# One MLP kernel, its first microseconds: x in two loads on two queues, w1's first half behind them, products by tiles

## The chip, the cores and the metric

The kernel runs on one core of a Trainium2 chip. The metric is the device time of one execution, in microseconds (us). Times are given as the median of several runs; the profile is of one further execution. Engines are named as in the profile: PE is TensorE's matmul and PEld its weight load, DVE is VectorE, ACT is ScalarE, POOL is GpSimd and SP is SyncE. A name with a q behind it (SPq, ACTq) is the engine's instruction stream, as it issues DMAs.

## The reference

```python
B, S, D, F = 1, 2048, 512, 1792        # bf16 inputs x, w1, b1, w2

def reference(x, w1, b1, w2):
    h = jnp.einsum("bsd,df->bsf", x, w1) + b1
    sp = jnp.log1p(jnp.exp(-jnp.abs(h))) + jnp.where(h > 0, h, jnp.zeros_like(h))
    act = h * jnp.tanh(sp)
    return jnp.einsum("bsf,fd->bsd", act, w2)
```

Two matrix products with a Mish activation between them: 2048 rows, 512 columns in, 1792 in the middle, 512 out.

## The kernel before

It is written by hand, engine by engine: each engine executes its instructions in the order in which the code issues them, and `Stream.wait` puts a semaphore wait ahead of an engine's next instruction. `load` issues one DMA with a semaphore of its own and returns the token to wait for; `load_w1` and `load_part` load columns of w1 for some of its four 128-row slices, k 0 to 3.

The 2048 rows are cut into four blocks of 512 (`BLOCKS`), a block into four tiles of 128 rows. The first product needs x with its columns on the partitions (`xT`). Its 512 columns are the four slices k, its 1792 outputs are fourteen slices f of 128. For block s and slice f, four matmuls (k 0 to 3) of 512 columns add up in one PSUM bank, ScalarE applies Mish with the bias and writes `a_sb` (`mish`, L160), and when a block's fourteen slices are done, `mm2` (L199) multiplies each of its four row tiles by w2 in fourteen matmuls; VectorE copies the result out of PSUM (L205) and SP stores it. The first products are those of L177.

Block 0 is started differently, and the change lies there. Of its four tiles, 2 and 3 come already transposed by a DMA (`t_x23`). Tiles 0 and 1 come as they are into `x_nat`, in one load of 256 KB from SP (`t_xn`), in which partition p holds rows 2p and 2p+1, so tile 0 holds the even rows and tile 1 the odd ones; the stores of these two tiles put them back (`rows`). TensorE transposes them in eight 128 x 128 pieces, tile by slice (`transpose_x`, L147), in four groups, each into a PSUM bank, and VectorE and ScalarE take turns to copy the groups into `xT` (L151).

Until x has landed, TensorE runs nine fillers (`WARM`, `dummy`, L130): matmuls of constants into a bank that nobody reads, five of 512 columns, three of 256 and one of 128. Behind the transposes come the products of slices f 0 to 3 (`F0` = 4) in banks 4 to 7, by `first(js, ks)` with row tiles js and slices ks:

```python
first((0,), (0,))
first((1,), (0,))
first((0, 1), range(1, KT))
first((2, 3), range(KT))
```

Each line runs over its ks, and within one k over the four slices f. Then follow slices 4 to 7 in two halves of k, each matmul 512 wide (`half`), and the rest.

The queues at the start: ScalarE issues w1's k 0-1 and k 2-3 for f 0 to 3 (256 KB each) ahead of its activation table; SP issues x, the DMA transpose of tiles 2 and 3, w1's columns for f 4 to 7 in two halves, b1, w1's columns for f 8 to 13, w2, and the DMA transposes of the other three blocks. A product waits for the load of its slice of w1 (`t_w1`) and for the copies or the DMA that made its part of `xT` (`t_cp`).

Of the kernel before, what the change touches and what calls it, by code (L numbers as in the profile page):

```python
# [4 lines left out]

P = 128
SQ = 32
WARM = (512,) * 5 + (256,) * 3 + (128,)
BLOCKS = (512, 512, 512, 512)


# [21 lines left out]
def bass_standalone__dense_activation_mish__prompt_kernel(  # L33
# [10 lines left out]
    BF, F32 = dt.bfloat16, dt.float32  # L44
# [3 lines left out]
    KT, FT = D // P, F // P  # L48
    assert (S, D, F) == (2048, 512, 1792) and sum(BLOCKS) == S
    x2, out2 = x[0], out[0]  # L50
# [3 lines left out]
    F0 = 4  # L54
    N0 = BLOCKS[0] // P

    with ExitStack() as es:
        def sb(name, shape, t):
            return es.enter_context(nc.sbuf_tensor(name, shape, t))

        x_nat = sb("x_nat", [P, 2, D], BF)
        xT = sb("xT", [P, KT, S], BF)
# [6 lines left out]
        ident = sb("ident", [P, P], BF)  # L69
        a_sb = sb("a_sb", [P, FT, S], BF)  # L70
        o_sb = sb("o_sb", [P, S // P, D], BF)
        ps = es.enter_context(nc.psum_tensor("ps", [P, 8, 512], F32))

        def sem(name):
            return es.enter_context(nc.semaphore(name))

        sp = Stream(nc.sync, None)
        pe = Stream(nc.tensor, sem("c_pe"))
        dve = Stream(nc.vector, sem("c_dve"))
        act = Stream(nc.scalar, sem("c_act"))  # L80
        pool = Stream(nc.gpsimd, sem("c_pool"))

        def load(q, dst, src, name, transpose=False):
            s = sem(name)
            (q.eng.dma_start_transpose if transpose else q.eng.dma_start)(dst, src).then_inc(s, 16)
            return (s, 16)

        def load_w1(q, ks, a, b):
            return load(q, w1_sb[:, ks, a * P:b * P], w1v[:, ks, a * P:b * P], "s_w1_%d_%d" % (ks.start, a))
# [5 lines left out]
        def load_part(q, k0, k1, a, b):  # L95
            t = load_w1(q, slice(k0, k1), a, b)
            for f in range(a, b):
                for k in range(k0, k1):
                    t_w1[k, f] = t

        t_bz = dve.mark(nc.vector.memset(b1_nat[:, :], 0.0))  # L101
        for k0, k1 in ((0, 2), (2, 4)):
            load_part(act, k0, k1, 0, F0)
        t_xn = load(sp, x_nat[:, :, :], x2[0:2 * P, :].rearrange("(p j) d -> p j d", p=P), "s_xn")
        t_x23 = load(sp, xT[:, :, 2 * P:4 * P], x2[2 * P:4 * P, :], "s_x23", True)
        for k0, k1 in ((0, 2), (2, 4)):
            load_part(sp, k0, k1, F0, 8)
# [3 lines left out]
        t = load(sp, w2_sb[:, :, :], w2v, "s_w2")  # L111
# [3 lines left out]
        for s in range(1, len(BLOCKS)):  # L115
            lo, hi = starts[s], starts[s + 1]
# [5 lines left out]
        t_id = pool.mark(pool.eng.affine_select(ident[:, :], ones[:, :], pattern=[[1, P]], compare_op=ALU.is_equal,  # L122
                                                fill=0.0, base=0, channel_multiplier=-1))
        act.eng.preload_act_table(ACT.Mish)  # L124

        c_w = nc.const_aps.tensor(1.0, [P, P], BF)
        c_m = nc.const_aps.tensor(1.0, [P, 512], BF)

        def dummy(n):
            nc.tensor.matmul(ps[:, 7, 0:n], c_w, c_m[:, 0:n], start=True, stop=True)  # L130


        free = [[] for _ in range(8)]
        t_cp = {(j, k): t_x23 for j in (2, 3) for k in range(KT)}
        t_mish, t_acc = {}, {}

        def transpose_x():

            pe.wait(t_xn, t_id)
            for bank, (eng, js, ks) in enumerate(((dve, (0,), (0,)), (act, (1,), (0,)), (dve, (0, 1), (1,)),  # L140
                                                  (act, (0, 1), (2, 3)))):
                n, m = len(ks), len(js)
                psb = ps[:, bank, 0:n * m * P // 2].bitcast(BF)
                for i, k in enumerate(ks):
                    for h, j in enumerate(js):
                        lo = (i * m + h) * P
                        mm = nc.tensor.transpose(psb[:, lo:lo + P], x_nat[:, j, k * P:(k + 1) * P], ident[:, :])  # L147
                eng.wait(pe.mark(mm))
                dst = xT[:, ks[0]:ks[0] + n, js[0] * P:(js[-1] + 1) * P]
                src = psb.rearrange("p (k t) -> p k t", k=n)  # L150
                t = eng.mark(nc.vector.tensor_copy(dst, src) if eng is dve else act.eng.activation(dst, src, ACT.Copy))  # L151
                for k in ks:
                    for j in js:
                        t_cp[j, k] = t
                free[bank] = [t]

        def mish(s, f, bank, t_mm):
# [7 lines left out]
        def mm1_step(s, f, k, bank, js=None):  # L165

            n = BLOCKS[s]
            lo, hi = (0, n) if js is None else (js[0] * P, (js[-1] + 1) * P)
            first = k == 0 and lo == 0
            if first:  # L170
                pe.wait(*free[bank])
            pe.wait(t_w1[k, f])
            if s:
                pe.wait(t_xT[s])
            else:
                pe.wait(*[t_cp[j, k] for j in (js or range(N0))])
            return nc.tensor.matmul(ps[:, bank, lo:hi], w1_sb[:, k, f * P:(f + 1) * P],  # L177
                                    xT[:, k, starts[s] + lo:starts[s] + hi], start=first, stop=(k == KT - 1 and hi == n))
# [6 lines left out]
        s_out = sem("s_out")  # L185
        n_out = 0

        def rows(i):

            if i < 2:  # L190
                return out2[0:2 * P, :].rearrange("(p j) d -> p j d", p=P)[:, i, :]
            return out2[i * P:(i + 1) * P, :]

        def mm2_step(i, f, lo, hi, bank):
            s = max(b for b in range(len(BLOCKS)) if starts[b] <= i * P)
            if f == 0:
                pe.wait(*free[bank])
            pe.wait(t_w2[f], t_mish[s, f])
            return nc.tensor.matmul(ps[:, bank, 0:hi - lo], a_sb[:, f, i * P:(i + 1) * P], w2_sb[:, f, lo:hi],  # L199
                                    start=(f == 0), stop=(f == FT - 1))  # L200

        def put(i, lo, hi, bank, t_mm):
            nonlocal n_out
            dve.wait(t_mm)
            t = dve.mark(nc.vector.tensor_copy(o_sb[:, i, lo:hi], ps[:, bank, 0:hi - lo]))  # L205
            free[bank] = [t]
            sp.wait(t)
            sp.eng.dma_start(rows(i)[:, lo:hi], o_sb[:, i, lo:hi]).then_inc(s_out, 16)
            n_out += 1

        def mm2(i, lo, hi, bank):
            for f in range(FT):
                mm = mm2_step(i, f, lo, hi, bank)
            put(i, lo, hi, bank, pe.mark(mm))


        def first(js, ks):
            for k in ks:
                for f in range(F0):
                    mm = mm1_step(0, f, k, 4 + f, js)  # L220
                    if k == KT - 1 and js[-1] == N0 - 1:
                        t_acc[f] = pe.mark(mm)
# [5 lines left out]
                if ks[-1] == KT - 1:  # L228
                    t_acc[f] = pe.mark(mm)

        for n in WARM:
            dummy(n)
        transpose_x()
        first((0,), (0,))
        first((1,), (0,))
        first((0, 1), range(1, KT))
        first((2, 3), range(KT))

        dve.wait(t_b1)
        for j in range(P // SQ):  # L240
            t = dve.mark(nc.vector.transpose(b1_T[j * SQ:(j + 1) * SQ, :], b1_nat[:, j * SQ:(j + 1) * SQ]))  # L241
# [52 lines left out]
```

## Time and profile before

| | |
|---|---|
| Runs (three) | 104.72 us median, 104.55 to 105.31 |
| Profiled execution | 105.42 us; span in the profile 104.1 us |
| PE | 101.5 us busy, 499 matmuls |
| ACT | 39.7 us busy; 48.0 us idle ahead of Mish, waiting for products |
| DVE | 12.8 us busy |
| DMA | 7.94 MB, 76 GB/s mean over the span |

A row of the timeline gives the start in us, the length in us, engine, line, operation, what is written and what is read, and how many instructions are merged (x8); in brackets the idle time ahead of them and what ended it. A row of the windows gives a stretch, its length, then the busy time and count of instructions of engines, the granted clock, the DMA engines' share and their GB/s. An answer on a tile has the line of each DMA that writes it, with its issue time in ns, its first and last issue in us, and the time from issue to landing.

### The profile page before, as it was taken

Reading aid. Unit: us, or ns where it says so; the run is one execution under the profiler, and the core shown is the slowest. Engines: PE = TensorE matmul, PEld = TensorE weight load, DVE = VectorE, ACT = ScalarE, POOL = GpSimd, SP = SyncE. Lnnn points to the kernel's source line nnn. Section 1 sums busy time; section 2 is a strip of 40 time slices with the busy share of each in tenths; the row PEclk is TensorE's granted clock in tenths of the full one; section 3 lists DMA queues with packets and bytes.
Section 4 is the critical chain, followed back from the end, with each engine's and each line's share of the span. In section 5 each row is a group of like instructions: output and inputs, shape, how many; then the busy total and the mean of one; then the engine's idle time right before and its main releaser. Section 6 shows DMA issues by size and latency. Waiting matters only on the chain.

```text
span 104.1 us, 1139 instructions
## 1 busy us (share of the span) xinstructions
PE 101.5 (97%) x499; PEld 48.8 (47%) x499; DVE 12.8 (12%) x25; ACT 39.7 (38%) x59; POOL 0.7 (1%) x6
## 2 busy tenths in 40 slices
PE   6999999999999999999999999999999999999992
PEld 2786444444444444444444444444444444444462
DVE  0103000022220000022220000022112000011223
ACT  3405997000027777200007777500005777700000
POOL 2000000000000000000000000000000000000000
PEclk9999999999999999999999999999999999999999
DMA  2999999681101000010111000001111000001111
GB/s 46 334 339 363 348 317 178 145 203 50 44 7 50 0 0 6 0 50 0 50 50 50 0 0 3 0 6 50 50 50 50 0 0 0 0 0 57 50 50 50
DMA packets 13345, 7.94 MB, mean 76 GB/s; under 512 B 7836, under 2 KB 13212, under 8 KB 13340
## 3 DMA queue, kind: packets, MB, share of 16 engines
q1 hardware_dynamic: 12796, 7.35, 27.1%
q10 hardware_dynamic: 544, 0.52, 1.4%
q8 instruction: 4, 0.07, 0.3%
q14 instruction: 1, 0.01, 0.0%
HBM read 3.94 MB, written 2.10 MB: 58 GB/s over the span
## 4 chain that ended last, share of the span: by engine, by line
PE 97%; DVE 0%; issue 0%
PE ps L177 47%; PE ps L199 46%; PE ps L130 3%; PE ps L147 1%; DVE o_sb L205 0%
## 5 line engine op out<-in xcount | busy, mean ns | idle before, releaser
L160 ACT ACTIVATE a_sb<-ps,b_sb 128x512 bf16<-128x512 f32 x56 | 37.5, 691 | 48.0 <-PE ps L177 48.0
L177 PE MATMUL ps<-xT,w_sb 128*128 128x512 bf16 (+2 forms) x244 | 49.8, 367 | 0.0
L199 PE MATMUL ps<-w_sb,a_sb 128*128 128x512 bf16 (+2 forms) x238 | 49.0, 366 | 0.0
L177 PEld LDWEIGHTS ps<-xT,w_sb 128*128 128x128 bf16 x244 | 24.2, 101 | 24.8
L199 PEld LDWEIGHTS ps<-w_sb,a_sb 128*128 128x128 bf16 x238 | 22.8, 98 | 25.9
L205 DVE CAST o_sb<-ps 128x512 bf16<-128x512 f32 (+2 forms) x17 | 11.2, 660 | 82.4 <-PE ps L199 82.4
L130 PE MATMUL ps<-const-bfloat16-1.0 128*128 128x512 bf16 (+2 forms) x9 | 3.0, 519 | 0.8 <-PEq L279 0.8
L130 PEld LDWEIGHTS ps<-const-bfloat16-1.0 128*128 128x128 bf16 x9 | 1.2, 138 | 2.3 <-issue 2.2
L124 ACT ACT_TABLE_LOAD x1 | 1.3, 1283 | 1.8 <-issue 1.8
L151 ACT ACTIVATE xT<-ps 128x128 bf16<-128x128 bf16 (+1 forms) x2 | 0.9, 437 | 1.4 <-PE ps L147 1.4
L241 DVE STREAM_TRANSPOSE b_T<-b_nat 32x32 bf16<-32x32 bf16 x4 | 0.8, 202 | 3.3 <-DMA b_nat<-in_b_dram 3.2
L147 PE MATMUL ps<-ident,x_nat 128*128 128x128 bf16 x8 | 1.0, 311 | 0.0
L151 DVE COPY xT<-ps 128x128 bf16<-128x128 bf16 (+1 forms) x2 | 0.5, 258 | 3.2 <-PE ps L147 3.1
L147 PEld LDWEIGHTS ps<-ident,x_nat 128*128 128x128 bf16 x8 | 0.8, 142 | 0.2 <-DMA x_nat<-in_x_dram 0.2
L122 POOL TENSOR_SCALAR_AFFINE_SELECT ident<-ones 128x128 bf16<-128x128 bf16 x1 | 0.3, 292 | 0.1
L101 DVE MEMSET b_nat<- 32x64 uint32 x1 | 0.1, 112 | 0.9 <-PEq L279 0.9
L120 POOL MEMSET ones<- 128x128 bf16 x1 | 0.2, 204 | 0.3 <-POOLq L279 0.3
L243 DVE CAST b_sb<-b_T 128x14 f32<-128x14 bf16 x1 | 0.2, 176 | 0.0
L279 POOL MEMSET const-bfloat16-1.0<- 128x1 bf16 x1 | 0.1, 101 | 0.0
L279 POOL MEMSET const-uint8-127<- 128x1 uint8 x1 | 0.1, 101 | 0.0
L279 POOL MEMSET const-float32-0.0<- 128x1 f32 x1 | 0.1, 98 | 0.3 <-issue 0.3
L279 POOL MEMSET const-float32-1.0<- 128x1 f32 x1 | 0.1, 99 | 0.0
## 6 DMA issues: line engine op xcount, KB each, us to landing
out_dram<-o_sb SPq DMA_DIRECT2D x15, 128.0 KB, 1.7
w_sb<-in_w_dram SPq DMA_DIRECT2D x1, 1792.0 KB, 10.3
w_sb<-in_w_dram SPq DMA_DIRECT2D x1, 768.0 KB, 5.5
w_sb<-in_w_dram ACTq DMA_DIRECT2D x2, 256.0 KB, 3.8
w_sb<-in_w_dram SPq DMA_DIRECT2D x2, 256.0 KB, 4.4
x_nat<-in_x_dram SPq DMA_DIRECT2D x1, 256.0 KB, 2.9
out_dram<-o_sb SPq DMA_DIRECT2D x1, 96.0 KB, 1.6
xT<-in_x_dram SPq DMA_TRANSPOSE x4, 5.9
```

Of the source, the lines that this page charges most:

```text
L120: t_ones = pool.mark(pool.eng.memset(ones[:, :], 1.0))
L122: t_id = pool.mark(pool.eng.affine_select(ident[:, :], ones[:, :], pattern=[[1, P]], compare_op=ALU.is_equal, fill=0.0, base=0, channel_mu ...
L124: act.eng.preload_act_table(ACT.Mish)
L130: nc.tensor.matmul(ps[:, 7, 0:n], c_w, c_m[:, 0:n], start=True, stop=True)
L147: mm = nc.tensor.transpose(psb[:, lo:lo + P], x_nat[:, j, k * P:(k + 1) * P], ident[:, :])
L151: t = eng.mark(nc.vector.tensor_copy(dst, src) if eng is dve else act.eng.activation(dst, src, ACT.Copy))
L160: t = act.mark(act.eng.activation(a_sb[:, f, starts[s]:starts[s + 1]], ps[:, bank, 0:n], ACT.Mish, bias=b1_sb[:, f:f + 1]))
L177: return nc.tensor.matmul(ps[:, bank, lo:hi], w1_sb[:, k, f * P:(f + 1) * P], xT[:, k, starts[s] + lo:starts[s] + hi], start=first, stop=( ...
L199: return nc.tensor.matmul(ps[:, bank, 0:hi - lo], a_sb[:, f, i * P:(i + 1) * P], w2_sb[:, f, lo:hi], start=(f == 0), stop=(f == FT - 1))
L205: t = dve.mark(nc.vector.tensor_copy(o_sb[:, i, lo:hi], ps[:, bank, 0:hi - lo]))
L241: t = dve.mark(nc.vector.transpose(b1_T[j * SQ:(j + 1) * SQ, :], b1_nat[:, j * SQ:(j + 1) * SQ]))
L279: nc = _bacc.Bacc("TRN2", target_bir_lowering=False, num_devices=1)
```

## The change

x's tiles 0 and 1 become two loads of 128 KB, rows 0 to 127 from SP and rows 128 to 255 from ScalarE. SP then issues w1's k 0-1 for f 0 to 3, and the DMA transpose third. ScalarE issues k 2-3 later, when the fourth filler (`HOLD` = 3, counted from 0) has finished. The fillers become five of 512 columns, one of 256 and two of 128. Each tile is transposed by itself when it is there, its slices 0 and 1 copied by VectorE, 2 and 3 by ScalarE. The products run over slices 0 and 1 of tile 0, then of tile 1, then over slices 2 and 3 of both. The rows of a tile are consecutive now, and `rows` goes.

```diff
-WARM = (512,) * 5 + (256,) * 3 + (128,)
+WARM = (512,) * 5 + (256,) + (128,) * 2
+HOLD = 3
...
-        for k0, k1 in ((0, 2), (2, 4)):
-            load_part(act, k0, k1, 0, F0)
-        t_xn = load(sp, x_nat[:, :, :], x2[0:2 * P, :].rearrange("(p j) d -> p j d", p=P), "s_xn")
+        t_xn = [load(q, x_nat[:, j, :], x2[j * P:(j + 1) * P, :], "s_xn%d" % j) for j, q in enumerate((sp, act))]
+        load_part(sp, 0, 2, 0, F0)
         t_x23 = load(sp, xT[:, :, 2 * P:4 * P], x2[2 * P:4 * P, :], "s_x23", True)
...
-        def transpose_x():
-
-            pe.wait(t_xn, t_id)
-            for bank, (eng, js, ks) in enumerate(((dve, (0,), (0,)), (act, (1,), (0,)), (dve, (0, 1), (1,)),
-                                                  (act, (0, 1), (2, 3)))):
...
+        def transpose_x(j):
+
+            pe.wait(t_xn[j], t_id)
+            for h, eng in enumerate((dve, act)):
+                bank = 2 * j + h
+                psb = ps[:, bank, 0:P].bitcast(BF)
+                for i in range(2):
+                    k = 2 * h + i
+                    mm = nc.tensor.transpose(psb[:, i * P:(i + 1) * P], x_nat[:, j, k * P:(k + 1) * P], ident[:, :])
                 eng.wait(pe.mark(mm))
-                dst = xT[:, ks[0]:ks[0] + n, js[0] * P:(js[-1] + 1) * P]
-                src = psb.rearrange("p (k t) -> p k t", k=n)
+                dst = xT[:, 2 * h:2 * h + 2, j * P:(j + 1) * P]
+                src = psb.rearrange("p (k t) -> p k t", k=2)
...
-            sp.eng.dma_start(rows(i)[:, lo:hi], o_sb[:, i, lo:hi]).then_inc(s_out, 16)
+            sp.eng.dma_start(out2[i * P:(i + 1) * P, lo:hi], o_sb[:, i, lo:hi]).then_inc(s_out, 16)
...
-        for n in WARM:
-            dummy(n)
-        transpose_x()
-        first((0,), (0,))
-        first((1,), (0,))
-        first((0, 1), range(1, KT))
+        for i, n in enumerate(WARM):
+            mm = dummy(n)
+            if i == HOLD:
+                act.wait(pe.mark(mm))
+                load_part(act, 2, 4, 0, F0)
+        transpose_x(0)
+        transpose_x(1)
+        first((0,), (0, 1))
+        first((1,), (0, 1))
+        first((0, 1), (2, 3))
         first((2, 3), range(KT))
```

More of the change, by code (lines that the diff above doesn't have):

```diff
@@ L129, in dummy @@
         def dummy(n):
-            nc.tensor.matmul(ps[:, 7, 0:n], c_w, c_m[:, 0:n], start=True, stop=True)
+            return nc.tensor.matmul(ps[:, 7, 0:n], c_w, c_m[:, 0:n], start=True, stop=True)
         free = [[] for _ in range(8)]
@@ L135, in bass_standalone__dense_activation_mish__prompt_kernel @@
         t_mish, t_acc = {}, {}
-        def transpose_x():
-            pe.wait(t_xn, t_id)
-            for bank, (eng, js, ks) in enumerate(((dve, (0,), (0,)), (act, (1,), (0,)), (dve, (0, 1), (1,)),
-                                                  (act, (0, 1), (2, 3)))):
[L142 to L147, printed above, removed]
+        def transpose_x(j):
[6 more added lines that the diff above has]
+                    mm = nc.tensor.transpose(psb[:, i * P:(i + 1) * P], x_nat[:, j, k * P:(k + 1) * P], ident[:, :])
                 eng.wait(pe.mark(mm))
-                dst = xT[:, ks[0]:ks[0] + n, js[0] * P:(js[-1] + 1) * P]
-                src = psb.rearrange("p (k t) -> p k t", k=n)
+                dst = xT[:, 2 * h:2 * h + 2, j * P:(j + 1) * P]
+                src = psb.rearrange("p (k t) -> p k t", k=2)
                 t = eng.mark(nc.vector.tensor_copy(dst, src) if eng is dve else act.eng.activation(dst, src, ACT.Copy))
-                for k in ks:
-                    for j in js:
-                        t_cp[j, k] = t
+                for i in range(2):
+                    t_cp[j, 2 * h + i] = t
                 free[bank] = [t]
@@ L186, in bass_standalone__dense_activation_mish__prompt_kernel @@
         n_out = 0
[L188 to L192, printed above, removed]
         def mm2_step(i, f, lo, hi, bank):
```

## The prediction

> **What bounds the kernel now.** I read the page first (span, engines, slices), then the chain of waits in order of time, then the timeline of the first ten microseconds with the DMA queues in it, because the diff touches nothing behind the first group of products.
>
> ```profile
> span 104.1 us, 1139 instructions
> PE 101.5 (97%) x499; PEld 48.8 (47%) x499; DVE 12.8 (12%) x25; ACT 39.7 (38%) x59; POOL 0.7 (1%) x6
> PE   6999999999999999999999999999999999999992
> ```
> ```profile
> 0.84 3.04 PE ps L130 x9
> 3.88 0.88 PE ps L147 x8
> 4.76 12.89 PE ps L177 x76
> 17.65 12.09 PE ps L199 x56
> ...
> 102.31 0.02 issue
> 102.33 0.29 DVE o_sb L205
> ```
>
> TensorE is the bound from 0.84 us to the end: the chain runs through nothing else but the last copy and store. It has three pieces at the start that do not belong to the large loops: nine fillers (3.04 us), eight transposes of x (0.88 us, 0.11 us each), and the first stage of products, 76 matmuls in 12.89 us. A 512-wide matmul of the loops takes 12.09 / 56 = 0.216 us. By columns, the 8 + 28 + 40 matmuls of the first stage would take 8 x 0.054 + 28 x 0.108 + 40 x 0.216 = 12.10 us, so this stage loses 0.79 us. It is not lost in waits but in rate:
>
> ```profile
> 2.08 0.15 PEld L130 LDWEIGHTS ps<-const-bfloat16-1.0 128*128 128x128 bf16 x1 [0.28 <-issue]
> 2.50 0.15 PEld L130 LDWEIGHTS ps<-const-bfloat16-1.0 128*128 128x128 bf16 x1 [0.28 <-issue]
> ```
> ```profile
> 5.40:6.05 0.65, 0.65 (x7) 0.47 (x4) 1.00 1.12 307
> 6.23:7.10 0.87, 0.87 (x10) 0.78 (x8) 1.00 1.11 347
> ```
>
> The first two rows are the weight loads that precede two 512-wide fillers: 0.42 us apart, twice 0.216. The second fence counts the products of L177 in two stretches (matmuls, then weight loads): three to four 256-wide ones in 0.65 us before 6.05, eight in 0.87 us after 6.23, that is 0.21 us each against 0.11. So TensorE runs at half rate until about 6.1 to 6.2 us and at full rate from there on. Both stretches print a granted clock of 1.00, so the spacing, not that column, shows it. What lies ahead of that moment is worth half: a product begun d earlier in the slow stretch has d more of half-rate time, which saves d/2 at the end.
>
> **What starts the first product.**
>
> ```profile
> 3.72 0.77 PEld L147 LDWEIGHTS ps<-ident,x_nat 128*128 128x128 bf16 x8 [0.22 <-DMA x_nat<-in_x_dram]
> 3.73 1.03 PE L147 MATMUL ps<-ident,x_nat 128*128 128x128 bf16 x8
> 4.05 0.61 DVE L151 COPY xT<-ps 128x128 bf16<-128x128 bf16 x2 [3.07 <-PE ps L147]
> ...
> 4.55 7.70 PE L177 MATMUL ps<-xT,w_sb 128*128 128x128 bf16 x51
> ```
> ```profile
> L85 SPq DMA_DIRECT2D x_nat<-in_x_dram x1: 396/396/396, 0.8 to 0.8; - x1
> ...
> DMA to landing us min/median/max: 2.9/2.9/2.9
> ```
> ```profile
> L85 ACTq DMA_DIRECT2D w_sb<-in_w_dram x2: 467/480/494, 0.8 to 1.3; - x2
> ...
> DMA to landing us min/median/max: 3.6/3.8/3.9
> ```
>
> x (256 KB) lands at 0.80 + 2.9 = 3.7, just as the fillers end, and the transposes start at 3.72. w1's k 0-1 (issued at 0.80, 256 KB) lands at 0.80 + 3.6 = 4.4, its k 2-3 at 1.3 + 3.9 = 5.2. The eight transposes stream until about 3.73 + 0.88 = 4.6, and the first product starts at 4.55: the transposes and w1's first half are ready within some 0.2 us of each other. That tie is the point of this case. Taking one of the two away uncovers the other.
>
> **The change part by part.** *Fillers.* Removed: 3 x 256 + 128 become 256 + 2 x 128 columns, 384 columns fewer, at 0.42 per 512 about 0.32 us. They now end at 3.72 - 0.32 = 3.40 or a little before.
>
> *x in two loads.*
>
> ```profile
> 1.80:2.50 0.70, 0.70 (x3) 0.15 (x1) 0.00 (x0) 0.68 (x1) 0.00 (x0) 1.00 0.89 126
> 2.50:3.10 0.60, 0.60 (x3) 0.29 (x2) 0.00 (x0) 0.60 (x1) 0.00 (x0) 1.00 0.95 321
> 3.10:3.70 0.60, 0.60 (x5) 0.29 (x2) 0.00 (x0) 0.00 (x1) 0.00 (x0) 1.00 1.07 377
> ...
> 4.40:5.40 1.00, 1.00 (x12) 1.00 (x10) 0.27 (x1) 0.63 (x2) 0.00 (x0) 1.00 1.23 278
> ```
>
> The last column is what the DMA engines moved: 126 GB/s in the first 0.7 us (88 KB), then 321 to 377 with the engines full. x's 262 thousand bytes are through at 2.50 + (262 - 88)/321 = 3.04 and land 0.66 later. Tile 0 alone would be through at 2.50 + (131 - 88)/321 = 2.63 and land at 3.3; if the two tiles share the engines evenly, at 3.7. I take 3.4, nearer to the first, because in the trace the load that was issued together with x, w1's, landed 0.7 after it, as a load does that is served second. Tile 1 then lands at 3.7, as x did. Its limit is what its four transposes hide behind: the four of tile 0, 0.43 us, run 3.42 to 3.85.
>
> *Transposes and copies.* Still eight, by tile: done at 3.85 + 0.43 = 4.28. The copies become four of 256 columns, two on VectorE and two on ScalarE, in place of 128, 256 / 128, 512. VectorE's two took 0.61 together and begin 0.32 after the first transpose; now the first one begins after two transposes, at about 3.42 + 0.43 = 3.85, and is done by 4.15, the second by 4.6. Tile 0's is ahead of 4.28, tile 1's ahead of the ninth product (below): nothing on the path.
>
> *w1's k 0-1.* Second on SP's queue instead of first on ScalarE's: issued at 1.25 instead of 0.80. That 0.45 costs nothing while the engines are still busy with x until 3.04. Then its bytes need 262/375 = 0.70: through at 3.74, landing with 0.66 of lag at 4.4, where it landed before. So the first product can be no earlier than about 4.4 + 0.1 = 4.50, whatever the fillers and transposes gain; TensorE idles from 4.28 to 4.4. The upper end, 4.7, is that a part of the 0.45 of later issue is passed on. The lower end is 4.30, from the transposes. Against 4.55 that is -0.25 to +0.15, and I take -0.05.
>
> *Products by tiles.* 16 x 128 + 8 x 256 columns instead of 8 x 128 + 12 x 256: the same 4096 columns, eight more instructions. In the half-rate stretch a 128-wide transpose takes 0.11, as columns say, so I cost them at nothing; the sixteen run 4.50 to 6.21.
>
> *k 2-3 behind the fourth filler.*
>
> ```profile
> 0.80 0.40 SPq L85 DMA_DIRECT2D x_nat<-in_x_dram  x1
> 1.25 1.30 SPq L85 DMA_TRANSPOSE xT<-in_x_dram  x1
> 1.82 1.28 ACT L124 ACT_TABLE_LOAD   x1 [1.82 <-issue]
> 2.62 1.08 SPq L85 DMA_DIRECT2D w_sb<-in_w_dram  x2
> ```
>
> ScalarE issues x's tile 1 until 1.27 and loads its table until 2.6, then waits. The fourth filler streams 2.08 to 2.50, and its result counts some 0.21 later (the copy at 4.05 begins 0.32 after a transpose that streams 0.11): the wait ends at 2.7, and the issue takes until 3.2. Queued behind it on ScalarE are only its copies, from 4.1 on. The transfer: x, w1's k 0-1 and, if served by issue, the DMA transpose of tiles 2 and 3 (issued from 1.25 + 0.48 = 1.75 to 3.05) are ahead. That transpose moves 262 thousand bytes at 278 GB/s, 0.94: through at 4.68; k 2-3 at 5.38. Such a load landed 0.8 behind its last bytes before (k 2-3: 3.74 + 0.70 = 4.44, landing 5.2), so 6.2. Mixed with the transpose it is 5.2 to 5.6 at best. It is wanted after the sixteen 128-wide products, at 6.21; before, after eight 128-wide and four 256-wide ones, at 4.55 + 16 x 0.11 = 6.3. So there is a wait of 0 to 0.1 at the one end and 0.6 to spare at the other, where there had been 1.0 of cover.
>
> *The DMA transpose third.*
>
> ```profile
> L85 SPq DMA_TRANSPOSE xT<-in_x_dram x1: 1305/1305/1305, 1.3 to 1.3; - x1
> ...
> DMA to landing us min/median/max: 4.9/4.9/4.9
> ```
> ```profile
> L85 SPq DMA_DIRECT2D w_sb<-in_w_dram x2: 464/516/568, 2.6 to 3.2; - x2
> ...
> DMA to landing us min/median/max: 4.3/4.4/4.4
> ```
>
> It landed at 6.2 and lands at 5.5 to 6.4, wanted from 6.21 + 8 x 0.11 = 7.1. Behind it on SP's queue everything is issued 0.5 later, but the bytes ahead are the same: the two loads of w1's columns 4 to 7 landed at 6.9 and 7.6 and are wanted from 8.7 and 10.4; a delay of 0.5 is covered more than three times. b1, w2 and the other transposes stand behind the same bytes.
>
> **The sum.** First product 0.05 earlier, worth 0.03; a wait for k 2-3 of 0 to 0.1 where the rate changes: together 0.0. The profiled execution took 105.42 us (span 104.1 and 1.3 around it), 0.7 above the median of the runs, so I carry the difference, not the level, over to the median: **104.7 us**.
>
> **The rivals.** *The tie breaks the other way* (w1 lands with or before the transposes, because its 0.45 of late issue lets x through sooner): first product at 4.30, 0.25 earlier, 0.13 off at half rate, 0.25 if the full rate comes after an amount of work and not at a moment: 104.5. For it: the engines are full only from 2.5 on. Against: the bytes ahead of w1's last are the same.
>
> *Tile 1 behind w1.* If ScalarE's ring is served after SP's two loads, tile 1 lands at 4.4, transposes end at 4.87, first product 4.95: 0.4 late, 0.2 to 0.4 on the end, 105.0. Against: ScalarE's k 2-3 moved ahead of SP's transpose, issued 0.04 sooner. *k 2-3 behind still more*: if columns 4 to 7 (2 x 262 thousand bytes at 350 GB/s, 1.5 us) pass it too, it lands at 7.7 and TensorE stands 1.5 us: 106.2; it decides once the landing passes 6.21. Same evidence against it.
>
> *The full rate comes later.* Before, it came after 5.3 us of work (0.84 to about 6.15) in which the chain of waits shows no break; now there are 0.1 to 0.3 us of idle at 4.3 and perhaps more at 6.2. If a break sends the count back, the rate doubles 5.3 us after 4.4, at 9.7 instead of 6.2: 3.5 us more at half rate, 1.75 on the end, 106.5, slower by 1.7%. It decides as soon as one break is too long; the one profile shows no break that was, nor one that was not. [...]
>
> **How the numbers follow.** Forecast 0.63; the tie the other way 0.16; tile 1 behind w1 0.10; k 2-3 far behind 0.04; the rate later 0.07. The three runs before lie 104.55 to 105.31 apart, so about 0.3 on either side of the median is not the change: the lower end is the gain's 104.5 less 0.2, 104.3, the upper one tile 1's 105.0 and 0.4, 105.4. About 1%, 1.05 us, is what a measurement of this kernel tells from no change; only the two cases above 106 reach it on the slow side, 0.04 + 0.07 = 0.11; on the fast side only the gain with the runs' scatter on top of it, 0.02; within it 0.87.
>
> **What would show it.** In the profile after: fillers end by 3.4; transposes begin at 3.4 to 3.5 and not 3.7; a wait of TensorE for w1's first load right ahead of the first product, at 4.5; weight loads 0.21 apart until 6.1 to 6.2 and then 0.11; k 2-3 landing at 5.2 to 6.2. A first product at 4.3 or at 4.95, or half-rate spacing beyond 7, would make the prediction wrong.

## The result and the profile after

| | before | changed |
|---|---|---|
| Runs (six each, on the same chip) | 105.02 us median, 104.55 to 105.39 | 110.40 us median, 109.44 to 111.26 |
| Ratio, 95% interval | | 1.048 (1.043 to 1.053) |
| Profiled execution | 105.42, span 104.1 | 110.77, span 109.5 |

The forecast was 104.7, the range 104.3 to 105.4; the changed kernel is 5.4 us slower than before. Ratios, here and below, count of each kernel the runs within 1.5% of its fastest one. The page of the changed kernel, first lines and slices:

```profile
span 109.5 us, 1146 instructions
PE 102.3 (93%) x502; PEld 48.9 (45%) x502; DVE 12.8 (12%) x25; ACT 39.7 (36%) x59; POOL 0.7 (1%) x6
PE   6714999999999999999999999999999999999993
PEclk9975599999999999999999999999999999999999
```

TensorE's busy time hardly changed, 102.3 for 101.5 us; the span grew around it. A slice is 2.7 us: the third one, 5.5 to 8.2, is nearly empty, and the granted clock is at half in slices four and five. The chain of waits in order of time (start, length, what) has a DMA in it now:

```profile
0.84 1.88 PE ps L131 x4
2.72 0.02 issue
2.74 6.82 DMA w_sb<-in_w_dram
9.56 0.05 issue
9.61 13.41 PE ps L175 x64
23.01 12.09 PE ps L191 x56
```

It runs through four fillers, the end of the wait on ScalarE at 2.74, the load of k 2-3 for 6.82 us, and only then through products. The timeline around it, and the load itself:

```profile
2.74 0.39 ACTq L86 DMA_DIRECT2D w_sb<-in_w_dram  x1
...
3.31 0.53 PEld L146 LDWEIGHTS ps<-ident,x_nat 128*128 128x128 bf16 x8
3.35 0.67 PE L146 MATMUL ps<-ident,x_nat 128*128 128x128 bf16 x8
...
4.73 1.07 PE L175 MATMUL ps<-xT,w_sb 128*128 128x128 bf16 x16 [0.71 <-DMA w_sb<-in_w_dram]
...
9.61 6.72 PE L175 MATMUL ps<-xT,w_sb 128*128 128x256 bf16 x33 [3.81 <-DMA w_sb<-in_w_dram]
```
```profile
L86 ACTq DMA_DIRECT2D w_sb<-in_w_dram x1: 385/385/385, 2.7 to 2.7; - x1
its engine sat idle before it (us, times) until:
who waited for it (us, times):
  PEld ps L175: 4.0, 1
...
DMA to landing us min/median/max: 6.8/6.8/6.8
```

The transposes' first weight load starts at 3.31, the first product at 4.73 after 0.7 us of idle, and the seventeenth at 9.61 after 3.81 by the row; the last of the first sixteen streams until 5.62. The windows (stretch, length, PE busy and count, granted clock, share of the DMA engines, GB/s) show both the rate of TensorE and that of the engines that bring the load:

```profile
4.72:5.62 0.90, 0.89 (x16) 1.00 0.94 162
5.70:6.80 1.10, 0.10 (x2) 1.00 1.00 321
6.90:9.50 2.60, 0.00 (x0) 0.50 1.03 365
9.60:13.60 4.00, 4.00 (x19) 0.50 1.09 359
13.80:15.80 2.00, 2.00 (x14) 1.00 2.06 252
```

A finer cut of the same view, without an engine's columns, has the rate of the DMA engines where k 2-3 starts to move:

```profile
4.40:4.90 0.50, 1.00 1.24 259
4.90:5.50 0.60, 1.00 0.85 118
5.50:6.50 1.00, 1.00 0.95 296
```

The sixteen 128-wide products took 0.056 us each, so TensorE had the full rate then, earlier than before; in the trace the spacing changes from 0.107 to 0.056 among the transposes, at about 3.5. While it stood idle the granted clock went to 0.50, and it came back between 13.6 and 13.8. So the first stage, 17.65 us at its end before and 23.02 now, divides as follows: the first product 4.73 - 4.55 = 0.18 later; the sixteen products at 0.89 instead of 16 x 0.107 = 1.71, 0.82 gained; idle from 5.62 to 9.61, 3.99 lost; and the other 64 products in 13.41 instead of 17.65 - 6.26 = 11.39, 2.02 lost, which is half of the 4.1 us at half rate. 0.18 - 0.82 + 3.99 + 2.02 = 5.37, the whole difference. Behind the first stage nothing changed: 12.09 per 56 products in both. This division is that of one execution. The 0.82 is not shown to come from the change: the run with more work in the wait (below) has the same program up to the sixteenth product, and there the spacing changes only at about 4.1. The 2.02 varies as well: of the six runs, the three with a mean granted clock of 0.969 over the span (the slow start prints as 1.00) took 110.8 to 111.3 us, and those at 0.984, 1.00 and 1.00 took 109.4 to 110.0.

### The profile page after: what moved, and what is told of

Same layout as the page of the kernel before. It is cut to its first block, busy times and chain, and to the rows that moved or that the text cites. A ratio compares the mean times of both kernels' runs of the same rounds, so it can differ in the third digit from the quotient of the medians.

```text
span 109.5 us, 1146 instructions
## 1 busy us (share of the span) xinstructions
PE 102.3 (93%) x502; PEld 48.9 (45%) x502; DVE 12.8 (12%) x25; ACT 39.7 (36%) x59; POOL 0.7 (1%) x6
## 4 chain that ended last, share of the span: by engine, by line
PE 91%; DMA 6%; DVE 0%; issue 0%
PE ps L175 45%; PE ps L191 44%; DMA w_sb<-in_w_dram 6%; PE ps L131 2%; DVE o_sb L197 0%
## 5 line engine op out<-in xcount | busy, mean ns | idle before, releaser
L175 PE MATMUL ps<-xT,w_sb 128*128 128x512 bf16 (+2 forms) x248 | 51.2, 370 | 4.5 <-DMA w_sb<-in_w_dram 4.5
L150 ACT ACTIVATE xT<-ps 128x256 bf16<-128x256 bf16 x2 | 0.7, 380 | 1.3 <-PE ps L146 1.3
L150 DVE COPY xT<-ps 128x256 bf16<-128x256 bf16 x2 | 0.5, 292 | 2.7 <-PE ps L146 2.7
```

## The experiments

Two theories stood at the start. Theory 1: k 2-3 comes to the DMA engines late, when SP's ring (its queue of DMAs) already has work for microseconds, and is kept back by sharing with it. Theory 2: a load on ScalarE's ring is held up by the DMA transpose in flight beside it. Ratios are against runs of the kernel before on the same chip, with 95% intervals. Each landing is read from one profile.

### Which part of the change costs the time

**The change without the hold, k 2-3 on SP ahead of the transpose.**

```diff
         load_part(sp, 0, 2, 0, F0)
+        load_part(sp, 2, 4, 0, F0)
         t_x23 = load(sp, xT[:, :, 2 * P:4 * P], x2[2 * P:4 * P, :], "s_x23", True)
...
-                act.wait(pe.mark(mm))
-                load_part(act, 2, 4, 0, F0)
```

> The changed kernel, but k 2-3 goes on SP's queue between k 0-1 and the DMA transpose; ScalarE's ring carries x's tile 1 alone. Both theories: k 2-3 lands near 5.3, no long wait, 104.5 to 105.4. It measures the rest of the change (x on two queues, fewer fillers, products by tiles) without the hold. If it is above 107 all the same, the hold is not the cause.

105.39 us median of ten, 105.13 to 105.75; ratio 1.002 (0.999 to 1.005). No difference: x on two queues, fewer fillers and products by tiles neither cost nor gain. The first product starts earlier than in either kernel, but k 2-3 landed at 1.73 + 4.3 = 6.0, not 5.3, and a short wait takes that back:

```profile
4.27 1.65 PE L176 MATMUL ps<-xT,w_sb 128*128 128x128 bf16 x16
6.07 6.20 PE L176 MATMUL ps<-xT,w_sb 128*128 128x256 bf16 x39 [0.15 <-DMA w_sb<-in_w_dram]
```

**The same load at once on ScalarE.**

```diff
+        load_part(act, 2, 4, 0, F0)
         load_part(sp, 0, 2, 0, F0)
...
-                act.wait(pe.mark(mm))
-                load_part(act, 2, 4, 0, F0)
```

> The changed kernel, but ScalarE issues w1's k 2-3 at once behind x's tile 1, at about 1.25 us, and does not wait for a filler. Theory 1 (k 2-3 comes to the DMA engines when SP's ring already has work for microseconds, and the two rings then share the engines): k 2-3 lands near 5.2 as before, no long wait, 104.5 to 105.4. Theory 2 (a load on ScalarE's ring in flight together with the DMA transpose is held up, whenever it was issued): k 2-3 still lands after 7 and the time stays above 107.

Ten runs fell in two groups, 105.08 to 105.76 and 106.94 to 107.80, five in each. The first group gives a ratio of 1.003 (0.999 to 1.007), as theory 1 has it. The profile is of the second group, so it explains only that one. k 2-3 landed at 5.7, and no product waited for it. With k 2-3 beside it, k 0-1 landed at 5.19, and the first product started at 5.23, 0.68 later than before:

```profile
5.23 13.94 PE ps L176 x80
```

The first stage ended at 19.18, 1.53 later than before. From its first product on it took 13.94, and 17.65 - 4.55 = 13.10 before, so 0.84 of the 1.53 was lost without a wait: in the trace the products stand at half-rate spacing until 8.6 here, and until 6.2 before. This is the prediction's rival "the full rate comes later", behind an idle time of 0.6 us; that this break is the reason is not shown.

**The same load on SP behind the transpose.**

```diff
         t_x23 = load(sp, xT[:, :, 2 * P:4 * P], x2[2 * P:4 * P, :], "s_x23", True)
+        load_part(sp, 2, 4, 0, F0)
...
-                act.wait(pe.mark(mm))
-                load_part(act, 2, 4, 0, F0)
```

> The changed kernel, but k 2-3 goes on SP's queue right behind the DMA transpose, issued at about 3.1 us, later than the 2.74 of the changed kernel. If the late issue as such costs the time: a landing at or after 9 and 109 or more. Theories 1 and 2 (the second ring is what matters): served in order behind the transpose, landing at 6.0 to 6.5, a wait of at most 0.5, 104.7 to 105.8.

106.43 us median of eight, 106.00 to 108.21; ratio 1.011 (1.007 to 1.015): slower, but by a quarter of the loss. Issued 0.35 later than in the changed kernel, it landed 2.3 earlier, so the moment of issue by itself is not the price. It was also 0.8 to 1.3 later than the 6.0 to 6.5 that its place among the bytes gave, which neither theory had:

```profile
L86 SPq DMA_DIRECT2D w_sb<-in_w_dram x1: 575/575/575, 3.1 to 3.1; - x1
...
DMA to landing us min/median/max: 4.2/4.2/4.2
```

**The hold alone, in the kernel before.**

```diff
-        for k0, k1 in ((0, 2), (2, 4)):
-            load_part(act, k0, k1, 0, F0)
+        load_part(act, 0, 2, 0, F0)
...
-        for n in WARM:
-            dummy(n)
+        for i, n in enumerate(WARM):
+            mm = dummy(n)
+            if i == 3:
+                act.wait(pe.mark(mm))
+                load_part(act, 2, 4, 0, F0)
```

> The kernel before, with one edit: ScalarE issues k 2-3 behind the fourth filler, as the changed kernel does. x in one load, nine fillers, products and the place of the DMA transpose stay. Theories 1 and 2: k 2-3 lands at 7 to 10 and the time is 107 to 111. If it stays within 1% of before, the hold needs another part of the change to hurt.

Four runs, 107.03 to 110.16; ratio 1.024 (1.014 to 1.034), which counts two of the four. In the profile, of the slowest run, k 2-3 landed at 2.74 + 5.3 = 8.05, TensorE waited 2.69 for it, and the clock went to half as in the changed kernel:

```profile
4.36 1.04 PE L176 MATMUL ps<-xT,w_sb 128*128 128x128 bf16 x12
8.10 4.24 PE L176 MATMUL ps<-xT,w_sb 128*128 128x256 bf16 x19 [2.69 <-DMA w_sb<-in_w_dram]
```

The four times follow the mean granted clock: 107.03 at 1.00, 108.51 and 108.78 at 0.984, 110.16 at 0.969. So the hold alone, without any other part, makes the kernel slower by 2 to 5 us, by the median of the four 3.6 of the 5.4. This, and the run with the load on SP ahead, settle which part it is; whether the rest of the change adds to it once the hold is there is not shown.

### Why the load takes so long

**No transpose beside it.** An ordinary load of the same bytes takes the DMA transpose's place.

```diff
-        t_x23 = load(sp, xT[:, :, 2 * P:4 * P], x2[2 * P:4 * P, :], "s_x23", True)
+        t_x23 = load(sp, x_alt[:, :, :], x2[2 * P:4 * P, :].rearrange("(j p) d -> p j d", p=P), "s_x23")
...
```

> The changed kernel, but tiles 2 and 3 come by an ordinary load of the same 256 KB into a buffer of their own in place of the DMA transpose, so their columns of block 0 are multiplied as zeros (the output of rows 256 to 511 is not the reference's). k 2-3 stays on ScalarE's ring behind the fourth filler. Theory 1 (sharing the engines with SP's stream is enough): k 2-3 still lands at 6.5 to 9.5, time 106.5 to 110.5. Theory 2 (the DMA transpose in flight beside another ring holds it up): k 2-3 lands by 6.0, time under 106. Since the ordinary load is issued faster than the transpose, SP's next loads come some 0.9 sooner, which by theory 1 makes it worse, by theory 2 changes nothing.

The columns of tiles 2 and 3 are zeros then. 110.8 us (two runs), ratio 1.056; k 2-3 landed at 2.74 + 7.1 = 9.8. Theory 2 falls: the transpose is not needed.

```profile
9.86 4.13 PE L177 MATMUL ps<-xT,w_sb 128*128 128x256 bf16 x24 [3.45 <-DMA w_sb<-in_w_dram]
```

**Nothing of SP's stream behind the transpose beside it.**

```diff
+        sp.wait(t_w1[2, 0])
         for k0, k1 in ((0, 2), (2, 4)):
             load_part(sp, k0, k1, F0, 8)
...
```

(All that SP issues behind the wait moves below the fillers with it.)

> The changed kernel, but SP waits until k 2-3 has landed before it issues anything behind the DMA transpose, so that ScalarE's ring shares the engines with the transpose alone. Theory 1 (the rest of SP's stream takes the engines' time): k 2-3 lands at 5.6 to 6.3, the wait ahead of the 17th product is under 0.5, and the later loads come some 3 us later, of which w1's columns 4 to 7 cost 0.5 to 1.5: 105.5 to 107. Theory 2: k 2-3 lands at 7 to 9.6 all the same, and the time is 110 or more.

109.9 us (two runs), ratio 1.047; k 2-3 landed at 2.74 + 5.7 = 8.5. Where SP waits, its later loads come late too (issued from 8.49), so only landings are read from such a run. Theory 1 falls as well, at least as it was put: with 256 KB of transpose and 256 KB of k 2-3 as the only transfers behind k 0-1 the load was late all the same. It cannot be the engines' bandwidth, as the windows show:

```profile
4.50:5.50 1.00, 0.19 (x4) 1.00 0.65 76
5.50:6.50 1.00, 0.93 (x16) 1.00 1.20 152
6.50:7.50 1.00, 0.00 (x0) 1.00 0.70 83
7.50:8.50 1.00, 0.00 (x0) 0.66 0.28 71
```

Last two columns: in the first three rows the engines count as 65 to 120% busy and move 76 to 152 GB/s, where they moved 321 to 377 in the kernel before. The packets themselves take longer: the 256 packets of k 2-3 (1 KB each) took 0.106 us on average here, and the packets of the same size on ScalarE's queue 0.046 in the kernel before.

**Nothing beside it.** SP holds the transpose too.

```diff
-        t_x23 = load(sp, xT[:, :, 2 * P:4 * P], x2[2 * P:4 * P, :], "s_x23", True)
...
+        sp.wait(t_w1[2, 0])
+        t_x23 = load(sp, xT[:, :, 2 * P:4 * P], x2[2 * P:4 * P, :], "s_x23", True)
...
```

> The changed kernel, but SP waits until k 2-3 has landed before it issues the DMA transpose and all that follows, so that ScalarE's load, issued at 2.74 as before, finds no other load behind w1's k 0-1. If a load that starts late is slow by itself (or because ScalarE's ring had run empty), k 2-3 lands at 7 or later. If it takes another transfer beside it, k 2-3 lands at 5.2 to 5.8, the sixteen products end near 6 and only the transpose, now issued at 5.5, is waited for (landing near 8.5): a wait of 1.5 to 2.5 and 107 to 108.5 in all.

Issued at the same 2.74, k 2-3 landed at 5.8: it takes another transfer beside it, as the second of the two expectations had it. The time, 109.1 (two runs, ratio 1.039), was above what was expected: the transpose landed at 9.2, and behind its wait of 2.22 us, which had been expected, TensorE was at half rate, which had not. The 23 products of 256 columns in the last row below took 0.22 each.

```profile
L86 ACTq DMA_DIRECT2D w_sb<-in_w_dram x1: 385/385/385, 2.7 to 2.7; - x1
...
DMA to landing us min/median/max: 3.0/3.0/3.0
```
```profile
4.00:4.50 0.50, 0.50 (x7) 1.00 0.47 68
4.50:5.50 1.00, 1.00 (x13) 1.00 0.65 220
...
9.24 5.08 PE L162 MATMUL ps<-xT,w_sb 128*128 128x256 bf16 x23 [2.22 <-DMA xT<-in_x_dram]
```

Even by itself the load starts slowly: 68 GB/s in its first full half microsecond.

**One ordinary load beside it.** As the run with SP held, with the ordinary load in the transpose's place.

```diff
-        t_x23 = load(sp, xT[:, :, 2 * P:4 * P], x2[2 * P:4 * P, :], "s_x23", True)
+        t_x23 = load(sp, x_alt[:, :, :], x2[2 * P:4 * P, :].rearrange("(j p) d -> p j d", p=P), "s_x23")
...
+        sp.wait(t_w1[2, 0])
...
```

> The run in which SP held everything behind the transpose until k 2-3 had landed (8.5), but again with an ordinary load in place of the transpose and zeros in its place (the output of rows 256 to 511 is not the reference's). Two ordinary loads of 256 KB, one on each ring, are left. If the transpose and ScalarE's ring hold each other up, k 2-3 lands at 5.2 to 6.0 here. If two rings at once are enough, at 7 or later. The later loads start when it has landed, so the time is 106 to 108 in the first case, 108.5 to 110.5 in the second.

107.3 us (two runs), ratio 1.022; k 2-3 landed at 2.74 + 4.1 = 6.8, between the two expectations. One ordinary load beside it costs about 1 us against 5.8, the transpose beside it 2.7, each by a single profile.

**One ring, no transpose.** As the run with k 2-3 on SP behind the transpose, with the ordinary load.

```diff
-        t_x23 = load(sp, xT[:, :, 2 * P:4 * P], x2[2 * P:4 * P, :], "s_x23", True)
+        t_x23 = load(sp, x_alt[:, :, :], x2[2 * P:4 * P, :].rearrange("(j p) d -> p j d", p=P), "s_x23")
         load_part(sp, 2, 4, 0, F0)
...
```

> The run with k 2-3 on SP's queue behind the transpose, but tiles 2 and 3 come by an ordinary load of the same size into a buffer of their own and are multiplied as zeros (the output of rows 256 to 511 is not the reference's). In that run k 2-3 landed at 7.3, 1.1 behind what its place among the bytes gave. If the transpose ahead of it is the reason, it lands at 5.6 to 6.2 here and the time is 105.0 to 105.6. If not, 6.8 or later and 106 or more.

106.25 us (two runs), ratio 1.012, k 2-3 landing at 7.1: no better than with the transpose ahead (7.3). The transpose is not the reason there either.

Put together, with the first and the last of the sixteen parts in which the trace records the landing of k 2-3 (updates of its semaphore). Sixteen is also the number of DMA engines that the page counts ("share of 16 engines"); whether each part is one engine's is not shown.

```
order of k 2-3                                       first part   last part
ScalarE, at once, behind k 0-1 (before)                 5.02         5.22
ScalarE, at once, behind k 0-1, x in two loads on SP    5.12         5.32
ScalarE, at once, behind x's tile 1                     5.52         5.70
ScalarE, held, nothing beside it                        5.33         5.79
SP, ahead of the transpose, all the rest behind it      4.75         6.03
SP, ahead of an ordinary load, all the rest behind it   4.65         6.18
ScalarE, held, one ordinary load beside it              5.32         6.80
SP, behind an ordinary load, all the rest behind it     5.32         7.06
SP, behind the transpose, all the rest behind it        6.18         7.30
ScalarE, held, transpose and all the rest (covered)     5.78         7.58
ScalarE, held, in the kernel before                     6.37         8.05
ScalarE, held, the transpose beside it                  6.27         8.47
ScalarE, held, transpose and all the rest (changed)     6.30         9.56
ScalarE, held, ordinary load and all the rest           6.70         9.81
```

The product that needs the load started behind the last part, in the changed kernel at 9.61 behind 9.56. With nothing beside it the parts landed within 0.5 us, in the changed kernel within 3.3: twelve by 7.20, the others at 7.63, 7.64, 8.09 and 9.56, and these set the time. SP's next two loads show the same there, landing last at 9.76 and 10.38 with fifteen of their sixteen parts in by 8.26 and 8.95, so what falls behind is not ScalarE's load alone. The two profiles with the same queues (covered and changed) differ by 2.0 us, so rows that lie closer than that are not told apart. What stands beyond it is that a held load landed later beside all the rest (9.56 and 9.81) or beside the transpose (8.47) than by itself (5.79), and that company alone does not do it: the loads of the first three rows had all of SP's stream beside them and were issued by 1.3. Why some parts fall behind, and why the packets take longer, is not settled by these runs.

### The clock

**Work in the wait.** Sixteen more fillers in a free bank ahead of the seventeenth product.

```diff
+        pe.wait(*free[3])
+        for _ in range(16):
+            nc.tensor.matmul(ps[:, 3, 0:512], c_w, c_m, start=True, stop=True)
         first((0, 1), (2, 3))
```

> The changed kernel with sixteen more 512-wide fillers ahead of the 17th product, where TensorE waits for k 2-3: 3.5 us of work in a wait of 3.8. If the idle stretch is what takes TensorE back to half rate, the full rate now stays and about 1.5 to 2.0 of the 5.4 come back: 108.4 to 109.2. If the rate depends on something else, the time is that of the changed kernel or more, 110 to 111.

108.17 us median of four, 107.86 to 108.46, ratio 1.032 (1.026 to 1.037): more work, 2.2 us less time than the changed kernel (1.7 by the two ratios), and a mean granted clock of 1.00 in all four runs, where four of the changed kernel's six are below. The chain has no DMA at that place any more, and the products behind the fillers ran at full rate:

```profile
4.32 1.04 PE ps L175 x16
5.36 3.50 PE ps L234 x16
8.86 2.62 PE ps L175 x24
```

24 products of 256 columns in 2.62 us are 0.109 each. The load landed at 7.6 in this profile, before the fillers ended at 8.86, so 1.3 us of them were not needed. Without the idle stretch the granted clock stayed at 1.00 from 4.3 to 11.5 in this profile, where it went to 0.50 inside the 3.99 us of the changed kernel's. The saving is near the 2.0 that the sum above put on the half rate, but k 2-3 also landed 2.0 earlier here than in the changed kernel's profile, so its size does not prove that share.

### Two attempts to beat both kernels

**k 2-3 on SP, an ordinary load between it and the transpose.**

```diff
         load_part(sp, 0, 2, 0, F0)
+        load_part(sp, 2, 4, 0, F0)
+        load_part(sp, 0, 2, F0, 8)
         t_x23 = load(sp, xT[:, :, 2 * P:4 * P], x2[2 * P:4 * P, :], "s_x23", True)
-        for k0, k1 in ((0, 2), (2, 4)):
-            load_part(sp, k0, k1, F0, 8)
+        load_part(sp, 2, 4, F0, 8)
...
-                act.wait(pe.mark(mm))
-                load_part(act, 2, 4, 0, F0)
```

> An attempt to beat both: the changed kernel without the hold, SP issues x's tile 0, w1's k 0-1, k 2-3, then the first half of columns 4 to 7, then the DMA transpose, then the second half; ScalarE's ring carries tile 1 alone. In the run with k 2-3 directly ahead of the transpose it landed at 6.0, although all but one of its loads ahead of other loads landed 0.4 to 0.7 behind their bytes. If the place ahead of a transpose is what delays the landing, k 2-3 lands at 4.8 to 5.2 here, no product waits for it, and the transpose is wanted at about 7.0 and lands at 6.8 to 7.4: 104.7 to 105.2. If not, 105.3 to 105.8.

106.22 us median of six, 105.42 to 106.62; ratio 1.011 (1.006 to 1.016). k 2-3 landed at 6.2, with an ordinary load behind it, and at 6.0 directly ahead of the transpose. But fifteen of its parts were in by 5.61 here, and there fifteen came from 5.83 on, so whether the place ahead of a transpose delays a load stays open. The transpose landed at 7.95, for which TensorE waited 0.71. A miss.

**The queues of before with the rest of the change.**

```diff
+        for k0, k1 in ((0, 2), (2, 4)):
+            load_part(act, k0, k1, 0, F0)
-        t_xn = [load(q, x_nat[:, j, :], x2[j * P:(j + 1) * P, :], "s_xn%d" % j) for j, q in enumerate((sp, act))]
-        load_part(sp, 0, 2, 0, F0)
+        t_xn = [load(sp, x_nat[:, j, :], x2[j * P:(j + 1) * P, :], "s_xn%d" % j) for j in range(2)]
...
-                act.wait(pe.mark(mm))
-                load_part(act, 2, 4, 0, F0)
```

> The other attempt to beat both: the queues of the kernel before (ScalarE: w1's k 0-1 and k 2-3 at once; SP: x, the transpose, the rest), but x as two loads on SP, the transposes and products by tiles, and the changed kernel's fewer fillers. The transposes start near 3.4, w1's k 0-1 lands at 4.2 to 4.4 as before and sets the first product at 4.4 to 4.5, 0.1 earlier than before, which is worth 0.05: 104.8 to 105.2, no difference that five rounds can show. Above 105.5 would mean that the smaller loads of x themselves cost something.

105.44 us median of twelve, 104.83 to 105.92; ratio 1.005 (1.002 to 1.007): slower by half a per cent. The profiled execution is the fastest of the twelve, 104.83, so it does not show where the half per cent goes. What it shows is that w1's first half landed ahead of x's tile 1, which came at 4.48, and that the second four transposes waited for it:

```profile
3.43 0.61 PE L147 MATMUL ps<-ident,x_nat 128*128 128x128 bf16 x4
4.53 0.40 PE L147 MATMUL ps<-ident,x_nat 128*128 128x128 bf16 x4 [0.49 <-DMA x_nat<-in_x_dram]
4.76 9.51 PE L176 MATMUL ps<-xT,w_sb 128*128 128x128 bf16 x67
```

This is the mechanism of the rival "tile 1 behind w1", in another order of queues. No version was faster than the kernel before.

## Why the prediction was wrong, step by step

- **The bound and the worth of the start: right.** TensorE bounds the kernel, and every microsecond at the start comes back at the end: the 5.37 us of the first stage are the 5.4 of the span. That half rate would last until 6.1 to 6.2, as before, was wrong: the full rate came at about 3.5, which gave 0.82 back by luck.
- **Fillers and x: right.** The fillers ended by 3.4 and the transposes started at 3.35 (3.42 was said). Tile 0 landed at 0.81 + 2.5 = 3.3, tile 1 at 0.80 + 2.6 = 3.4, 0.3 earlier than said.
- **w1's k 0-1 and the first product: just past the upper end.** It landed at 4.68 (4.4 was said) and the first product started at 4.73; the forecast was 4.50 with 4.7 as the bound. That the gain of fillers and x is uncovered by this load was right; it cost 0.18.
- **k 2-3 behind the fourth filler: this step failed.** The end of the wait was right, 2.74 for 2.7. The landing was put at 5.2 to 6.2 and was 9.56. The step took rates from the kernel before, 278 to 375 GB/s, and laid the loads end to end; the trace of before shows those rates only for loads that were queued early, each behind the other. The rates of the changed kernel fall to 118 GB/s between 4.9 and 5.5, and the last part of k 2-3 lands 2.4 us behind the twelfth. The bound for an unknown was drawn from one side only: "mixed with the transpose" was taken to be the faster case, 5.2 to 5.6, and with the transpose alone beside it k 2-3 landed at 8.47. The step did name that the cover of 1.0 us was gone, and that was the warning to widen the range by.
- **The DMA transpose third: right; the later loads: wrong, without a price.** The transpose landed at 1.73 + 3.9 = 5.6 (5.5 to 6.4 was said). The two loads of w1's columns 4 to 7 were to come 0.5 later than their 6.9 and 7.6; they landed at 9.76 and 10.38, 2.8 later. In the timing of before they are wanted from 8.7 and 10.4; that no product waited for them is due to TensorE being late itself.
- **The rival "k 2-3 behind still more" is nearest to what happened,** 1.5 us of standing at a chance of 0.04; w1's columns 4 to 7 went beside k 2-3, though, and landed behind it. The rival was too small, 3.99 instead of 1.5, and too unlikely, because its evidence against (ScalarE's loads had been served ahead of SP's transpose) came from loads issued at the same moment.
- **The rival on the rate came with it,** not instead of it. Its mechanism was not a break of 0.1 to 0.3 us ahead of the first product: behind the 0.7 us there the products ran at full rate. The rate fell in the idle time of 3.99 us behind the sixteenth product, where the granted clock went to 0.50, and the price was 2.0 in the profiled execution (1.75 was said). Counting the two as alternatives left their sum, about 108, without a chance of its own.
- **Products by tiles at nothing: right.** The run with k 2-3 on SP ahead of the transpose has all of this and no hold, and its interval holds 1.

The moment of the full rate shifts from order to order: with fillers that start at 0.84 in each, the spacing of the matmuls changes at about 3.5 in the changed kernel, at 5.5 in the run with k 2-3 on SP ahead, whose sixteen products took 1.65 us where the changed kernel's took 1.07, and at 8.6 in the run with k 2-3 at once on ScalarE. What sets it is not shown. The later half rate of the changed kernel lasted from between 6.8 and 6.9 until between 13.6 and 13.8, about 6.8 us. A shorter idle time than its 3.99 was followed by half rate too: one wait of 2.22 us (nothing beside it). In the changed kernel the granted clock fell 1.2 us after the last product, and in the run with SP held inside the wait of 2.1 us, visible as 0.66 in its last row; both had another break of 0.7 to 0.8 us shortly before.

## What to carry to other kernels

Holding back a transfer so that others get ahead gives up its cover, and what it then took could not be summed up here from the rates of a trace in which everything was queued early: a load that had 1 us to spare became 2.7 to 4.0 us late by being issued 1.4 us later. When a change moves a load's issue, price its landing from the slowest company seen, and ask what the wait would do to the matmul clock as well: here the two losses added, 3.99 us of idle time and 2.02 of half rate. To see what is worth trying, split the change first: here one run without the hold and one with the hold alone told which part it was.

## What the runs showed of the hardware that was not expected

- A 256 KB load issued at 2.74 landed 3.0 us later with nothing beside it, 4.1 beside one ordinary load of 256 KB, 5.7 beside one DMA transpose of the same size, and 4.8 to 7.1 beside all of SP's stream (one profile each). Beside the transpose the DMA engines counted as 65 to 120% busy for 3 us while moving 76 to 152 GB/s.
- The sixteen parts of one load landed up to 3.3 us apart (6.30 to 9.56).
- With no other load behind w1's k 0-1, the DMA engines moved 68 GB/s from 4.0 to 4.5, when k 2-3 started, and 220 GB/s from 4.5 to 5.5.
- One idle time of 2.22 us (nothing beside the load) was followed by half rate, 0.22 us for a product of 256 columns; in the changed kernel half rate lasted about 6.8 us, 4.1 of them under work.
- With the same program up to that point, the full rate came at about 3.5 us in one profile and at about 4.1 in another; in a third order of loads it came at 8.6.
